# Attention and two MoE layers in one program: second copies of q and k made by transfers, and four more weights converted in the third token block

## The chip, the cores and the metric

One Trainium2 chip, one core. The metric is the device time of one execution of the program in microseconds (us). TensorE (PE) multiplies; VectorE (DVE), ScalarE (ACT) and GpSimd (POOL) do elementwise work; SyncE (SP) issues every transfer of this kernel, in the order in which they stand on its queue.

## The reference

```python
def _attn_ref(q, k, v, f):                      # 4 batches, 8 heads, 576 tokens, 64 wide
    scores = scale * np.matmul(q, k.transpose(0, 1, 3, 2))
    cum = np.cumsum(np.log(np.clip(f, 0.0001, 1.0)), axis=-1)
    scores = np.where(causal, -1e9, scores + cum[..., :, None] - cum[..., None, :])
    ...
    return np.matmul(attn, v)
def _moe_ref(x, w_in, w_out):                   # 2304 tokens, 512 -> 2048 -> 512
    h = x @ w_in
    return (h * np.clip(h + 3.0, 0.0, 6.0) / 6.0) @ w_out
def _moe2_ref(x, w_in, w_out):
    h = x @ w_in
    g = np.maximum(h, 0.0) + np.log1p(np.exp(-np.abs(h)))
    return g @ w_out
```

The output is the second MoE of the first MoE of the attention. The weights of both MoEs arrive as 64-bit floats, so each 128x512 piece of them is loaded as two 32-bit words an element (512 KB) and converted on the chip to float32.

## The kernel before

**Precision.** Most products run in the faster rounded format (fp32r): an operand is split into a rounded part and a rest, and three products (rounded x rounded, rounded x rest, rest x rounded) are summed. For the scores of attention the split is laid out along the partitions: tile QA holds 64 rows of rounded q and 64 rows of its rest; KA holds rounded k twice; KB holds the rest of k, and QB once more the rounded q, each with rows for the decay. One score product is KA x QA plus KB x QB. So the rounded q must stand in QA and in QB, and the rounded k must stand twice in KA: these are the second copies.

**Attention.** Heads go in 16 pairs, two heads (0 and 1) to a pair. The first four pairs use plain float32 (`whole`); from the fifth on `qk_job` (L588) makes the split for a pair: VectorE transposes the raw tile (L599), ScalarE rounds each head (`hi`, L629), VectorE makes the rest (`lo`, L632), and `dup` (L638 to L645) makes the second copy: by a transfer (L641), on ScalarE (L643) or on VectorE (L645). The tiles of the seventh to the sixteenth pair are one set (`z` is 0), so a pair's head is rounded only when the same head of the pair before has had its scores. Then `s_job` multiplies (L685), VectorE finds the row minimum (L701), ScalarE takes exponentials (L710), TensorE transposes them (L776), and `pv_job` multiplies by v (L846).

**First MoE.** Tokens go in blocks of 512 (the fifth has 256); each block runs through 16 slices `ft` of the hidden width, with `moe1_g1` (L1296), the activation (ScalarE L1336, VectorE L1338, the split of its result L1316 or L1317 and L1319) and `moe1_g2` (L1359). Blocks one to three run on TensorE between the pieces of attention; blocks four and five run together after attention has ended.

**Second MoE.** It works with sums of quarter matrices (seven products in place of eight): `step_a` (L1412) and `step_b` (L1513). Its weights have to be converted from 64 bits (ScalarE L1017, VectorE L1019 and L1020), summed (L1104), and split (ScalarE L1133, GpSimd or VectorE L1136) before. Some of them are converted early, in blocks two and three of the first MoE, by `early2`, and stored to `wf_dram` (L1070); the table `early` (L1563) says which goes with which slice. In blocks four and five `weights2` loads these as float32 (L1088, 256 KB); those not in the table are loaded raw (L1002, 512 KB) and converted there.

**What sets the order.** Each operation is an `Op` with one or more ways (an engine and a cost), a due time `at`, and what it depends on. `Work.order` (L148) takes them one by one: on each engine the one that can start first, and of ways the one that would end first. It writes the order of all queues, so a change of one operation's ways moves others. Every engine then works through its queue in order. For `dup` the three ways carry a surcharge: 2800 ns for the transfer, 469.53 ns on ScalarE, none on VectorE.

Of the kernel before, what the change touches and what calls it, by code (L numbers as in the profile page):

```python
# [48 lines left out]
    NZ=6,  # L49
# [56 lines left out]
class Work:  # L106
# [11 lines left out]
    def op(self, ways, fn=None, r=(), w=(), after=(), at=0.0, banks=(), hold=(), free=(), nbytes=0, name="", seq=None, from_=0.0, rows=1.0):  # L118


        o = Op()
        o.ways = [ways] if isinstance(ways, tuple) else list(ways)
        o.at, o.banks, o.hold, o.free, o.nbytes, o.name = at, list(banks), hold, free, nbytes, name
        o.deps, o.succ, o.est, o.eng = {}, [], 1000.0 * from_, None
        o.early, o.rows = self.mark, rows
        for b in o.banks:
            b.users += 1
        r, w = list(r) + o.banks, list(w)
        for t in r:
            if t in self.writer:  # L130
                o.deps[self.writer[t]] = 1
        for t in w:
            for d in [self.writer.get(t)] + self.readers.get(t, []):
                if d is not None:
                    o.deps.setdefault(d, 1)
        for t in after:
            for d in [self.writer.get(t)] + self.readers.get(t, []):
                if d is not None:
                    o.deps.setdefault(d, 0)
        if seq:  # L140
            if seq in self.writer:
                o.deps.setdefault(self.writer[seq], 0)
            self.writer[seq] = o
        for t in r:
            self.readers.setdefault(t, []).append(o)
        for t in w:
            self.writer[t] = o
            self.readers[t] = []  # L148
        self.ops.append(o)
        return o  # L150
# [123 lines left out]
def attention_two_moe_kernel(  # L274
# [19 lines left out]
    B, H, S, D = q.shape  # L294
    NT, DM = out.shape
    NC = DM // P
    NF = moe_w_out.shape[0] // P
# [32 lines left out]
    op = wk.op  # L330
# [6 lines left out]
    def act(n, psum, extra=0):  # L337
        return 0.833 * n + (50 if psum else 93) + 93 * extra

    def dve(n, fast=False, extra=0):  # L340
        return (0.52 if fast else 1.04) * n + 67 + 61 * extra
# [10 lines left out]
    def dma(fn, nbytes, n=1, **kw):  # L352
        return op(("sp", 520.0 * n, fn), nbytes=nbytes, **kw)
# [9 lines left out]
    def moe_at(t, ft):  # L363

        t = min(t, LAST_B - 1)
        return BLK[t] + (BLK[t + 1] - BLK[t]) * (ft / NF) ** (K["cA"] if t == 0 else 1.0)
# [44 lines left out]
    NE, NS, NZ = K["NE"], K["NS"], K["NZ"]  # L411
# [91 lines left out]
    def qz(n):  # L503

        return (NZ - n) % 2 if n < NZ else 0
# [83 lines left out]
    def qk_job(b, hp, nm, at):  # L589

        pn = b * HP + hp
        whole = pn < NS
        z = qz(pn)
        tz = 1 if pn < NZ and nm == "kr" else 0
        x = "Q" if nm == "qr" else "K"
        A = x + "A"
        if not whole:
            wk.mark = ("w",) if tz else ()
            op(("dve", dve(S), lambda: nc.vector.transpose(T["t"][tz], raws[nm])), r=[(nm, 0), (nm, 1), "early"], w=[("t", tz)], at=at, name="T" + x)  # L599
        wk.mark = ("s", "w") if whole else ("w",) if z or tz else ()  # L600
        new = ["early", "set1"] if z and not whole else ["early"]
        for i in range(2):
            a, c = (0, D) if i == 0 else (D, 0)
            bh = b * H + 2 * hp + i
            if whole:
                op(("dve", dve(S), lambda i=i, a=a: nc.vector.transpose(T[x][i][0:D], raws[nm][a:a + D])),
                   r=[(nm, i), "early"], w=[(x + "F", i)], at=at, name=f"T{x}{i}")

                def row(i=i):
                    o = D if nm == "qr" else D + 32  # L610
                    return T[x][i][o:o + 1]

                def cum(bh=bh):
                    return T["vr"][cz].rearrange("p j h d -> p (j h d)")[bh:bh + 1, 0:S] if bh < 2 else cum_dram[bh:bh + 1]

                if bh == 0:
                    op([("act", act(S, False), lambda: nc.scalar.activation(out=row(0), in_=cum(0), func=ACTF.Copy)),
                        ("dve", dve(S, True), lambda: nc.vector.tensor_copy(row(0), cum(0)))],
                       r=["early", ("vr", cz)], w=[(x + "Fd", i)], at=-1.5, name="dec0")
                else:  # L620
                    dma(lambda row=row, cum=cum: nc.sync.dma_start(out=row(), in_=cum()), 4 * S,
                        r=["early", ("vr", cz) if bh < 2 else "cum"], w=[(x + "Fd", i)], at=at - K["xl"], name="dec")
                continue

            def to(y, o, i=i):
                return T[x + y][z][i][o:o + D]

            def hi(a=a, to=to):
                nc.scalar.activation(out=to("A", a), in_=T["t"][tz][a:a + D], func=ACTF.Copy)  # L629

            def lo(a=a, c=c, to=to):
                nc.vector.tensor_tensor(  # L632
                    to("A", c) if nm == "qr" else to("B", 0), T["t"][tz][a:a + D], to("A", a).bitcast(F32), op=ALU.subtract)

            op(("act", act(S, False), hi), r=new + [("t", tz)], w=[(A, z, i)], at=at, name=f"{A}{i}hi")
            op(("dve", dve(S), lo), r=[("t", tz), (A, z, i)], w=[("QAl" if nm == "qr" else "KB", z, i)], at=at, name=f"{A}{i}lo")

            def dup(e, a=a, c=c, to=to):  # L638
                o, y = to("B", 0) if nm == "qr" else to("A", c), to("A", a).bitcast(F32)
                if e is nc.sync:  # L640
                    e.dma_start(out=o.bitcast(F32), in_=y)  # L641
                elif e is nc.scalar:
                    e.activation(out=o, in_=y, func=ACTF.Copy)  # L643
                else:
                    e.tensor_copy(o, y)  # L645

            def dec(i=i, bh=bh):
                o = T["QB"][z][i][D:D + 2] if nm == "qr" else T["KB"][z][i][D + 2:D + 4]
                nc.sync.dma_start(out=o.bitcast(F32), in_=dec_dram[bh])

            ways = [("sp", 520.0, lambda f=dup: f(nc.sync), 2800.0),
                    ("act", act(S, False), lambda f=dup: f(nc.scalar), K["dupa"]),
                    ("dve", dve(S, True), lambda f=dup: f(nc.vector), K["dupd"])]
            op(ways, nbytes=4 * D * S, r=[(A, z, i)], w=[("QB" if nm == "qr" else "KAl", z, i)], at=at, name=f"dup{A}{i}")
            dma(dec, 8 * S, r=["dec"] + new, w=[(x + "Bd", z, i)], at=at - K["xl"])

    def s_job(pn, i, idx, at):
# [264 lines left out]
    def attention():  # L922
# [5 lines left out]
        for nm in ("qr", "kr"):  # L928
            qk_job(*specs[0], nm, 0.0)
            load_qk(nm, *specs[1], K["lq1"])  # L930
        prev = None
        for n in range(len(specs) + 1):
            for i in range(2):
# [26 lines left out]
                if i == 1 and n + 1 < len(specs):  # L960
                    for nm in ("qr", "kr"):
                        qk_job(*specs[n + 1], nm, when(0.95))
                        if n + 2 < len(specs):
                            load_qk(nm, *specs[n + 2], when(1.0))
# [595 lines left out]
        for o in range(2):  # L1560
            weights(o, ft, moe_at(0, ft) - K["cv"] + o * 2)

    early = {(1 + n // 8, n % 8 * 2): (1, n) for n in range(NF)} | {(1 + n // 4, n % 4 * 2 + 9): (0, n) for n in range(NF // 2)} if wide else {}  # L1563
    late2 = [(o, ft) for o in range(2) for ft in range(NF) if wide and (o, ft) not in early.values()]
    units = [(t, ft) for t in range(NB - 2) for ft in range(NF)]
    units += [(t, ft) for ft in range(NF) for t in (NB - 2, NB - 1)]
    for n in range(len(units) + 1):
        if n < len(units):
            t, ft = units[n]
            if (t, ft) == (NB - 2, 0):  # L1570
# [3 lines left out]
                at = moe_at(t, 0) - K["xl"]  # L1574
# [6 lines left out]
            if ft == NF - 1 and t + 1 < NB - 1:  # L1581

                at = moe_at(t + 1, 0) - K["xl"]
# [85 lines left out]
```

## Time and profile before

| | us |
|---|---|
| runs | 1009.79, 1010.3, 1008.93; median 1009.79 |
| the profiled execution | 1006.66 |
| its span, first to last instruction | 1004.7 |
| busy in the span: TensorE | 972.6 |
| VectorE | 801.8 |
| ScalarE | 590.1 |
| GpSimd | 249.2 |

The granted clock of TensorE is 1.00 (2.4 GHz) in all stretches shown below. Where the stages lie: the first MoE's block one is written out (L1387, L1388) at 240 to 245 us, block two at 369 to 372, block three at 486 to 498, blocks four and five at 625 to 629; `step_a` (L1412) runs from 628 to 820 and `step_b` (L1513) from 812 to 999. The last pair of heads is normalized (L879) at 472. How to read a page: busy time is the time in which an engine had an instruction; idle time counts only on the engine that sets the end, here mostly TensorE; a wait row says which instruction ended an idle time. TensorE's instructions overlap, so their mean duration is longer than the step from one to the next.

### The profile page before, as it was taken

To read this page: it belongs to the slowest core of one execution; us is meant where nothing else is said; L and a number is where in the kernel's file an instruction comes from. 1 tells how busy PE (TensorE), PEld (TensorE's weight loads), DVE (VectorE), ACT (ScalarE), POOL (GpSimd) and SP (SyncE) were. 2 spreads that over 40 slices of the span, in tenths; PEclk is the share of its full clock that TensorE was granted. 3 is DMA by queue.
4 is the path that set the end of the run, shared out by engine and by line. 5 is a ranking of instruction groups with operands and counts; after the bars stand their busy time and mean duration, and the time that the engine had idled before them with its cause. 6 is when DMAs were issued, how large, how long until landed. Compare 5 with 4: busy or idle time off the path is not lost.

```text
span 1004.7 us, 17646 instructions
## 1 busy us (share of the span) xinstructions
PE 972.6 (97%) x6116; PEld 847.3 (84%) x6116; DVE 801.8 (80%) x1615; ACT 590.1 (59%) x1295; POOL 249.2 (25%) x242
## 2 busy tenths in 40 slices
PE   8998999999999999999999999999999999999997
PEld 6565777778888788888888887899999999999997
DVE  8789878898989777886685876878787768888885
ACT  6998777777676556774344545655565544343342
POOL 2222232310000100000454642210010317554442
PEclk9999999999999999999999999999999999999999
DMA  6775544554654426542664751543425994444442
GB/s 139 171 189 150 141 129 117 144 142 99 169 153 162 100 88 180 147 132 83 215 213 145 251 163 46 170 167 132 143 103 197 332 354 125 125 143 134 124 121 72
DMA packets 192065, 153.46 MB, mean 153 GB/s; under 512 B 108220, under 2 KB 163932, under 8 KB 191080
## 3 DMA queue, kind: packets, MB, share of 16 engines
q1 hardware_dynamic: 191976, 152.34, 50.7%
q8 instruction: 48, 0.79, 0.3%
q14 instruction: 41, 0.34, 0.1%
HBM read 99.68 MB, written 52.47 MB: 151 GB/s over the span
## 4 chain that ended last, share of the span: by engine, by line
PE 69%; DVE 16%; issue 4%; DMA 4%; ACT 2%; POOL 2%; SPq 1%; DVEq 0%; POOLq 0%; ACTq 0%
PE bank L1513 16%; PE bank L1296 14%; PE bank L1412 14%; PE bank L1359 13%; PE bank L685 5%; PE bank L846 4%; PE bank L776 4%; DVE MX L1319 2%; DVE GT L1338 1%; DMA st<-in_moe_w_in_dram 1%; DVE p L701 1%; DVE st L1020 1%; SPq L535 1%; DMA st<-in_moe_w_out_dram 1%; DVE KB L632 1%
## 5 line engine op out<-in xcount | busy, mean ns | idle before, releaser
L1296 PE MATMUL bank<-MX,W 128*128 128x512 f32 x768 | 224.2, 402 | 9.1 <-DVE GT L1338 6.0
L1359 PE MATMUL bank<-MX,W 128*128 128x512 f32 (+1 forms) x688 | 186.3, 380 | 0.0
L1296 PEld LDWEIGHTS bank<-MX,W 128*128 128x128 f32 x768 | 132.1, 189 | 31.0 <-DVE GT L1338 7.7
L1359 PEld LDWEIGHTS bank<-MX,W 128*128 128x128 f32 x688 | 121.5, 188 | 22.1 <-DVE MX L1319 0.3
L1513 PE MATMUL bank<-rW,rW 128*128 128x256 f32 x1134 | 138.7, 283 | 1.4 <-POOL rW L1136 0.8
L1513 PEld LDWEIGHTS bank<-rW,rW 128*128 128x128 f32 x1134 | 136.8, 191 | 2.2 <-POOL rW L1136 1.0
L1412 PE MATMUL bank<-XO,rW 128*128 128x288 f32 x672 | 92.8, 298 | 3.0 <-DVE HY L1430 1.2
L1412 PEld LDWEIGHTS bank<-XO,rW 128*128 128x128 f32 x672 | 90.3, 188 | 4.9 <-DVE rBW L1430 1.8
L710 ACT ACTIVATE p<-p,stats 64x64 f32<-64x64 f32 (+4 forms) x130 | 72.0, 555 | 31.5 <-DVE stats L701 30.7
L1492 ACT ACTIVATE rW<-st 128x512 fp32r<-128x512 f32 (+1 forms) x72 | 36.9, 518 | 77.3 <-PE bank L1513 50.9
L1336 ACT ACTIVATE GT<-bank,three 128x512 f32<-128x512 f32 x80 | 51.4, 643 | 37.0 <-DVE MX L1319 16.2
L1412 PE MATMUL bank<-MX,rW 128*128 128x288 f32 x480 | 70.2, 297 | 1.3 <-DVE HY L1430 1.0
L1412 PEld LDWEIGHTS bank<-MX,rW 128*128 128x128 f32 x480 | 65.8, 188 | 2.1 <-DVE HY L1430 1.2
L1033 POOL TENSOR_TENSOR W<-st,W 128x512 fp32r<-128x512 f32 x24 | 33.2, 1387 | 135.3 <-ACT W L1032 118.8
L581 POOL TENSOR_TENSOR V<-vr,V 128x640 fp32r<-128x640 f32 x10 | 16.3, 1629 | 195.9 <-ACT V L577 168.5
L1319 DVE TENSOR_TENSOR MX<-GT,MX 128x512 fp32r<-128x512 f32 (+1 forms) x69 | 53.7, 784 | 11.5 <-ACT MX L1316 10.8
L1496 POOL TENSOR_TENSOR rW<-st,rW 128x256 fp32r<-128x256 f32 (+1 forms) x35 | 42.1, 1206 | 79.7 <-ACT rW L1492 61.7
L1338 DVE SCALAR_TENSOR_TENSOR GT<-GT,bank 128x512 f32<-128x512 f32 x80 | 49.9, 629 | 14.3 <-ACT GT L1336 13.3
L701 DVE CUSTOM_DVE_ANT_0 p<-bank,bar 64x64 f32<-64x64 f32 (+4 forms) x130 | 51.6, 421 | 11.4 <-PE bank L685 10.1
L776 PEld LDWEIGHTS bank<-ident,p 128*128 128x128 f32 x390 | 46.6, 140 | 14.7 <-DVE ptl L816 1.6
L811 ACT ACTIVATE pth<-bank 128x320 fp32r<-128x320 f32 (+2 forms) x100 | 42.3, 432 | 27.5 <-PE bank L776 21.4
L776 PE MATMUL bank<-ident,p 128*128 128x128 f32 x390 | 57.7, 274 | 0.6 <-ACT p L730 0.2
(215 smaller groups left out, 2042.4 us busy)
## 6 DMA issues: line engine op xcount, KB each, us to landing
st<-g_dram SPq DMA_DIRECT2D x36, 512.0 KB
st<-in_moe_w_out_dram SPq DMA_DIRECT2D x32, 512.0 KB
st<-in_moe_w_in_dram SPq DMA_DIRECT2D x30, 512.0 KB
wo_dram<-XO SPq DMA_DIRECT2D x49, 256.0 KB
g_dram<-HY SPq DMA_DIRECT2D x16, 576.0 KB
g_dram<-rBW SPq DMA_DIRECT2D x16, 576.0 KB
rW<-wo_dram SPq DMA_DIRECT2D x5, 1792.0 KB
wf_dram<-st SPq DMA_DIRECT2D x24, 256.0 KB
```

Source lines behind the costliest of these rows:

```text
L685: nc.tensor.matmul(acc[:r, o:o + c - a], qs[:, q0:q0 + r], ks[:, a:c], start=(n == 0 and ti == todo[-1][0]), stop=(n == len(ops) - 1), ski ...
L701: nc.vector.tensor_tensor_reduce(out=T["P"][par][ti][:r, a:c], in0=bank[bk.i][:r, o:o + c - a], in1=bar[:r, b0:b0 + c - a], op0=ALU.add, o ...
L710: nc.scalar.activation(out=pt, in_=pt, func=ACTF.Exp, scale=-1.0, bias=sv[:r, 0, ti:ti + 1], accum_out=sv[:r, 1, ti:ti + 1],)
L776: nc.tensor.transpose(acc[:, p0:p0 + P], T["P"][par][ti][:, k0:k0 + P], ident)
L811: nc.scalar.activation(out=place("PTH", j, ks, a, c), in_=src(), func=ACTF.Copy)
L1296: nc.tensor.matmul(bank[bk.i][:, 0:n], w[:, c], x[:, c, 0:n], start=(c == 0 and p == 0), stop=(c == NC - 1 and p == 2))
L1319: op(("dve", dve(n), lambda: nc.vector.tensor_tensor(t(glt), g, t(ght).bitcast(F32), op=ALU.subtract)), r=[("g", i), ("gh", i3)], w=[("gl" ...
L1336: op(("act", act(n, True, 1), lambda: nc.scalar.activation(out=g, in_=bank[bk.i][:, 0:n], func=ACTF.Relu, bias=three)), r=["three"], banks ...
L1338: op(("dve", dve(n), lambda: nc.vector.scalar_tensor_tensor(out=g, in0=g, scalar=6.0, in1=bank[bk.i][:, 0:n], op0=ALU.min, op1=ALU.mult)), ...
L1359: nc.tensor.matmul(bank[b][:, o:o + n], w[:, c * P:(c + 1) * P], x, start=(ft == 0 and p == 0 and o == 0), stop=(ft == NF - 1 and p == 2), ...
L1412: nc.tensor.matmul(bank[bks[b].i][:, 0:HA], wa[u][:, c], xa[v][:, c], start=(nm in ("P1", "P2", "P5") and c == 0 and y == 0), stop=(c == 1 ...
L1513: nc.tensor.matmul(bank[bks[b].i][:, o * 256:(o + 1) * 256], ga[u], wa[v], start=(p == 0 and o == 0 and y == 0), stop=(p == NPR - 1 and y ...
```

## The change

```diff
@@ qk_job, ways of dup @@
             ways = [("sp", 520.0, lambda f=dup: f(nc.sync), 2800.0),
                     ("act", act(S, False), lambda f=dup: f(nc.scalar), K["dupa"]),
                     ("dve", dve(S, True), lambda f=dup: f(nc.vector), K["dupd"])]
-            op(ways, nbytes=4 * D * S, ...)
+            op(ways if pn < NZ else ways[:1], nbytes=4 * D * S, ...)
@@ table of early conversions @@
-    early = {(1 + n // 8, n % 8 * 2): (1, n) for n in range(NF)} | {(1 + n // 4, n % 4 * 2 + 9): (0, n) for n in range(NF // 2)} if wide else {}
+    early = {(1 + n // 8, n % 8 * 2): (1, n) for n in range(NF)} | {(1 + (n + 4) // 8, (n + 4) % 8 * 2 + 1): (0, n) for n in range(3 * NF // 4)} if wide else {}
```

`NZ` is 6, so from the seventh pair of heads on the second copies have the transfer as their only way. The built program has 40 of these transfers in place of one; the copies on VectorE fall from 39 to 8 (those of pairs five and six), those on ScalarE from 8 to none. The table now has twelve first weights in place of eight: numbers 8 to 11 are new, and 4 to 7 stay in block three. Block three then has 16 conversions in place of 12, one with each slice, and blocks four and five have four in place of eight.

Other work moves along with this. In the first block four activation splits go from ScalarE (L1316) to VectorE (L1317), and in blocks four and five seven weight rests go from GpSimd to VectorE (L1136), while two weight sums (L1104) go the other way.

VectorE's queue at the ninth pair, before (QB_164 and KA_165 are the second copies of q, head 1, and k, head 0; GT is the first MoE's activation):

```order
L632 TENSOR_TENSOR QA_162<-qkt_169,QA_162 64x576
L645 CAST QB_164<-QA_162 64x576
L599 STREAM_TRANSPOSE qkt_169<-kr 128x576
L861 TENSOR_TENSOR xs<-bank_76,xs 64x256
L1338 SCALAR_TENSOR_TENSOR GT<-GT,bank_71 128x512
L632 TENSOR_TENSOR KB_167<-qkt_169,KA_165 64x576
L645 CAST KA_165<-KA_165 64x576
L632 TENSOR_TENSOR KB_168<-qkt_169,KA_166 64x576
```

The same place now:

```order
L632 TENSOR_TENSOR QA_162<-qkt_169,QA_162 64x576
L861 TENSOR_TENSOR xs<-bank_76,xs 64x256
L599 STREAM_TRANSPOSE qkt_169<-kr 128x576
L861 TENSOR_TENSOR xs<-bank_75,xs 64x320
L725 TENSOR_SCALAR stats_149<-stats_149 128x10
L726 RECIPROCAL stats_149<-stats_149 128x10
L632 TENSOR_TENSOR KB_167<-qkt_169,KA_165 64x576
L1019 TENSOR_SCALAR st_170<-st_170 128x512
L632 TENSOR_TENSOR KB_168<-qkt_169,KA_166 64x576
L1020 SCALAR_TENSOR_TENSOR st_170<-st_170 128x512
L1338 SCALAR_TENSOR_TENSOR GT<-GT,bank_71 128x512
```

Both copies are gone, and the activation L1338 of that slice stands behind the rests of k and a weight conversion.

SyncE's queue at the eighth pair now, a piece of the difference (L649 loads decay rows, L1002 loads raw weights, L733 stores the row sums, L535 loads the next pair's k; the rows marked + stood elsewhere or are new):

```order
+L649 DMA QB_164<-dec_dram 2x576
+L649 DMA KB_168<-dec_dram 2x576
+L641 DMA QB_164<-QA_162 64x576
+L1002 DMA st_170<-in_moe_w_in_dram 128x4x256
 L733 DMA inv_dram_93<-p_152 10x128
+L535 DMA kr<-in_k_dram 32x18x32 x4
+L1002 DMA st_171<-in_moe_w_out_dram 128x1024
+L641 DMA KA_165<-KA_165 64x576
+L641 DMA KA_166<-KA_166 64x576
 L745 DMA ivb<-inv_dram_93 64x64
```

The copies of k stand behind the loads of the next k and behind a weight load that waits for its staging buffer.

VectorE's queue in blocks four and five, a piece of the difference (st_170 is a staging buffer of a weight that was converted here before):

```order
 L1136 TENSOR_TENSOR XO<-XT,XO 128x256
-L1019 TENSOR_SCALAR st_170<-st_170 128x512
-L1020 SCALAR_TENSOR_TENSOR st_170<-st_170 128x512
 L1338 SCALAR_TENSOR_TENSOR GT<-GT,bank_71 128x256
 L1104 TENSOR_TENSOR XT<-XO 128x256
 L1319 TENSOR_TENSOR SB<-GT,SB 128x512
```

The two instructions of a conversion that stood between a weight rest and the activation are gone.

## Rows read from the trace of the kernel before

**Rows 1.** Stretches: us; busy us (instructions) PE, PEld, DVE, ACT, POOL; clock; DMA share; GB/s
```profile
105.00:245.00 140.00, 134.73 (x703) 105.51 (x702) 117.41 (x265) 103.93 (x234) 32.98 (x23) 1.00 0.48 129
245.00:480.00 235.00, 232.92 (x1273) 194.24 (x1272) 192.95 (x467) 150.46 (x347) 12.79 (x8) 1.00 0.49 138
480.00:628.00 148.00, 142.15 (x789) 120.77 (x788) 108.86 (x163) 66.64 (x146) 66.85 (x74) 1.00 0.53 170
```

**Rows 2.** TensorE's waits, 105 to 245 us: total us, times, longest us
```profile
PE bank L1296 <- DVE GT L1338: 3.3, 2, 2.0
```

**Rows 3.** TensorE's waits, 480 to 628 us
```profile
PE bank L1296 <- DVE GT L1338: 4.7, 7, 1.8
```

**Rows 4.** Second copies, groups by line, 105 to 440 us: xcount | busy us, mean ns
```profile
L645 DVE CAST QB<-QA 64x576 fp32r<-64x576 f32 x16 | 8.3, 521 | 0.2
L645 DVE CAST KA<-KA 64x576 fp32r<-64x576 f32 x15 | 6.8, 454 | 0.3
```

**Rows 5.** VectorE in order of time at the ninth pair: start, us, instruction
```profile
197.24 1.56 DVE L645 CAST QB<-QA 64x576 fp32r<-64x576 f32 x1
...
200.09 0.69 DVE L1338 SCALAR_TENSOR_TENSOR GT<-GT,bank 128x512 f32<-128x512 f32 x1
```

**Rows 6.** TensorE in order of time there: in brackets, idle before and what ended it
```profile
200.84 0.96 PE L1296 MATMUL bank<-MX,W 128*128 128x512 f32 x3 [1.35 <-DVE GT L1338]
```

**Rows 7.** GpSimd in order of time there
```profile
197.17 1.32 POOL L1033 TENSOR_TENSOR W<-st,W 128x512 fp32r<-128x512 f32 x1 [0.46 <-ACT W L1032]
```

**Rows 8.** VectorE in order of time at the eighth pair
```profile
163.24 0.45 DVE L645 CAST KA<-KA 64x576 fp32r<-64x576 f32 x1
...
165.50 0.69 DVE L1338 SCALAR_TENSOR_TENSOR GT<-GT,bank 128x512 f32<-128x512 f32 x1
```

**Rows 9.** VectorE in order of time, blocks four and five
```profile
558.40 1.03 DVE L1020 SCALAR_TENSOR_TENSOR st<-st 128x512 uint32<-128x512 uint32 x1
559.36 0.41 DVE L1338 SCALAR_TENSOR_TENSOR GT<-GT,bank 128x256 f32<-128x256 f32 x1
```

**Rows 10.** TensorE in order of time, blocks four and five
```profile
559.82 0.62 PE L1296 MATMUL bank<-SB,W 128*128 128x256 f32 x3 [0.86 <-DVE GT L1338]
...
582.38 0.96 PE L1296 MATMUL bank<-MX,W 128*128 128x512 f32 x3 [0.70 <-DVE GT L1338]
```

**Rows 11.** Weight conversions, groups by line, 320 to 480 us
```profile
L1020 DVE SCALAR_TENSOR_TENSOR st<-st 128x512 uint32<-128x512 uint32 x14 | 9.6, 683 | 0.4
L1019 DVE TENSOR_SCALAR st<-st 128x512 uint32<-128x512 uint32 x14 | 5.9, 419 | 0.1
```

**Rows 12.** Weight rests on VectorE, group by line, whole span
```profile
L1136 DVE TENSOR_TENSOR XO<-XT,XO 128x256 fp32r<-128x256 f32 x13 | 9.7, 752 | 0.0
```

**Rows 13.** ScalarE, then SyncE, in order of time at the one copy by transfer
```profile
344.54 0.69 ACT L629 ACTIVATE QA<-qkt 64x576 fp32r<-64x576 f32 x1 [3.09 <-PE bank L685]
...
345.32 0.51 SPq L641 DMA_DIRECT2D QB<-QA  x1
```

**Rows 14.** Transfers, 345.3 to 347.9 us, busy tenths in 40 slices of 0.065 us
```profile
DMA  0002000000000000009699689896410000000000
```

**Rows 15.** ScalarE rounding k, twelfth and sixteenth pair (two heads a row)
```profile
295.63 1.37 ACT L629 ACTIVATE KA<-qkt 64x576 fp32r<-64x576 f32 x2
...
434.61 1.39 ACT L629 ACTIVATE KA<-qkt 64x576 fp32r<-64x576 f32 x2 [0.16 <-DVE qkt L599]
```

**Rows 16.** TensorE, first scores of head 0 of these two pairs
```profile
299.14 0.39 PE L685 MATMUL bank<-KA,QA 128*128 128x192 f32 x2
...
441.19 0.37 PE L685 MATMUL bank<-KA,QA 128*128 128x192 f32 x2
```

**Rows 17.** The chain of waits, 150 to 215 us: raw weight loads, from issue to landing
```profile
154.00 4.33 DMA st<-in_moe_w_out_dram
...
162.35 3.86 DMA st<-in_moe_w_in_dram
```

**Rows 18.** SyncE's waits, whole span
```profile
SPq L1002 <- POOL W L1033: 21.0, 13, 5.2
```

More of the change, by code (lines that the diff above doesn't have):

```diff
@@ L653, in qk_job @@
                     ("dve", dve(S, True), lambda f=dup: f(nc.vector), K["dupd"])]
-            op(ways, nbytes=4 * D * S, r=[(A, z, i)], w=[("QB" if nm == "qr" else "KAl", z, i)], at=at, name=f"dup{A}{i}")
+            op(ways if pn < NZ else ways[:1], nbytes=4 * D * S, r=[(A, z, i)], w=[("QB" if nm == "qr" else "KAl", z, i)], at=at, name=f"dup{A}{i}")
             dma(dec, 8 * S, r=["dec"] + new, w=[(x + "Bd", z, i)], at=at - K["xl"])
```

## The prediction

> **What bounds the kernel now.** I read the stretches first. From 105 us on the change acts; the reader is to see that TensorE is busy nearly all of each stretch, so only its idle time can be won: 140.00 - 134.73 = 5.3 us from 105 to 245, 235.00 - 232.92 = 2.1 us from 245 to 480, 148.00 - 142.15 = 5.9 us from 480 to 628 [rows 1]. VectorE is busy 117.41 of the first 140 us: it is the next engine there. Then I read who ends TensorE's idle time. In the first stretch 3.3 us are two waits for the activation L1338 on VectorE [rows 2], in the last 4.7 us are seven such waits [rows 3]. So the first-MoE activation, late on VectorE, is what TensorE waits for where it waits at all; in the middle stretch, where attention's later half runs, there is almost nothing to wait for. Last I looked for what stands ahead of L1338 in VectorE's order of time.
>
> **The change, part by part.** The sum is made against the profiled execution, 1006.66 us; the median of the runs, 1009.79, stands 3.1 us above it, and I add that at the end.
>
> *Copies that leave VectorE.* From 105 us on VectorE makes 16 + 15 = 31 second copies, 8.3 + 6.8 = 15.1 us [rows 4]; all go. (ScalarE's eight go too; no wait of TensorE named in rows 2 or 3 ends on ScalarE, so I price them at nothing.) What counts is a copy ahead of a late L1338. There are two. At the ninth pair a copy of 1.56 us stands two short instructions ahead of L1338 [rows 5], and L1338 ended 1.35 us of idle time [rows 6]: without the copy the whole wait can go. At the eighth pair a copy of 0.45 us stands one instruction ahead of L1338 [rows 8], which ended the longest wait, 2.0 us [rows 2]: 0.45 can go. I take 1.35 + 0.45 = 1.8 us. The ends are 0, since the planner fills the room (four activation splits of the first block move onto VectorE, about 4 x 0.45 = 1.8 us by the nearest row, a cast [rows 4], and in the new order other work stands ahead of L1338), and 5.3, all the idle time of the stretch.
>
> *The middle stretch.* VectorE loses copies and gains four conversions of 0.683 + 0.419 = 1.10 us [rows 11], 4.4 us, beside as many on ScalarE. All of it lies beside TensorE, which is idle 2.1 us here; I take a gain of 0.3, with ends 0 and 2.1. What hides the conversions is that VectorE is busy 192.95 of 235 us [rows 1]; with that cover gone each would cost its 1.10. The four transfers in and four out lie on queues whose DMA share is 0.49 [rows 1]; nobody waits for them until block four.
>
> *Four conversions that leave blocks four and five.* Two of their instructions stand just ahead of an L1338: 1.03 us before the L1338 of 559.36 [rows 9], which ended 0.86 us of idle time, and another ahead of the wait of 0.70 [rows 10]. That is 1.56 us of waits that lose their cause. But seven weight rests come onto VectorE in the same blocks, 7 x 0.752 = 5.3 us by the nearest row [rows 12], and the conversions that leave are worth 4 x 1.10 = 4.4 at their usual price [rows 11]; VectorE's sum does not fall. I take half, 0.8 us. Ends: a loss of 5.3 - 4.4 = 0.9, and 4.7, all waits for L1338 [rows 3]. Loads of 256 KB in place of 512 KB are worth nothing more, since no wait in rows 3 ends on a transfer.
>
> *What the copies cost as transfers.* The trace has one. Its source was rounded by 344.54 + 0.69 = 345.23; SyncE issued it at 345.32 and spent 0.51 us [rows 13]; its packets ended in the 30th slice of 0.065 us, at 347.25 [rows 14]: 2.0 us after the rounding, with the queues idle otherwise. Is that in time? The tightest is the first k copy, head 0: at the twelfth pair it is rounded at 295.63 + 1.37/2 = 296.3 [rows 15] and its scores start at 299.14 [rows 16], 2.8 us later; at the sixteenth pair 435.3 and 441.19 leave 5.9. Ten copies are of this kind; the other thirty are made a pair's head earlier than they are read. So an undisturbed copy costs TensorE nothing. Behind a raw weight load it does: such a load takes 4.33 or 3.86 us from issue to landing [rows 17], and the copy's own packets 12 slices, 0.8 us [rows 14], so up to 5.1 us, 2.3 too late at the twelfth pair and in time at the sixteenth. I take 0.5 us for all ten, with ends 0 and 2.3. SyncE's 39 x 0.51 = 20 us of issuing lie beside its waits; loads stand queued well ahead of their use, and if that cover goes it is the third rival below.
>
> *Sum.* 1.8 + 0.3 + 0.8 - 0.5 = 2.4 us less: 1004.3 against the profiled execution, and 1007.4 as a median of runs.
>
> **A rule against the first term.** The copy at 197.24 took 1.56 us, while the copies of k take 0.454 on average [rows 4], and GpSimd worked on a weight rest from 197.17 for 1.32 us [rows 7]. The Trainium skill (GPSIMD Engine Reference, section 1, Specifications) says that GpSimd shares its SBUF interface with VectorE and contends with VectorE instructions that run in a two-port mode or have two SBUF inputs. The row agrees: the lengthening came while GpSimd worked. That makes a rival, the second below, since 1.1 of the 1.56 us would not leave with the copy but pass to the next VectorE instruction.
>
> **The rivals.**
> First, *the idle time only moves*. The planner rewrites all queues: of the waits that I remove, some other instruction is late next (a weight conversion or the rests of k, which now stand ahead of L1338). For it: VectorE is 84% busy from 105 to 245 [rows 1], and TensorE's order moves too. Against: 15.1 us less on VectorE. Time: no change, 1009.8.
> Second, *the lengthening passes on*: the ninth pair's wait shrinks by the copy's usual 0.45 in place of 1.35 [rows 4, 6], the first term is 0.9, the sum 1.5 us: 1008.3.
> Third, and slower: *the k copies come late by SyncE's queue*. In the new order a raw weight load stands directly ahead of the first k copy at four of the ten pairs (the eighth, twelfth, thirteenth and sixteenth), and such a load waits for GpSimd to give its staging buffer back: 21.0 us in 13 waits, 1.6 each, at most 5.2 [rows 18]. The copy would then land 1.6 + 4.33 + 0.8 = 6.7 us after the rounding: 3.9 too late at the twelfth pair and 0.8 at the others if they have the sixteenth's room, 3.9 + 3 x 0.8 = 6.3 us of TensorE's time. Against the gains of 2.9 that is 3.4 us slower: 1013.2. It decides once the copies are late by 2.9 + 2.0 = 4.9 us together. For it: TensorE works in order, and the middle stretch has no other idle time to hide this in. Against: the new TensorE order puts the scores later at such pairs, and buffers are often free.
> That the change does not do what it says is no rival: the new queues show 40 transfers, and four raw loads fewer in blocks four and five.
>
> **How the numbers follow.** A measurement of this kernel can tell about 0.2%, 2.0 us, from no change, so faster is below 1007.8 and slower above 1011.8. Forecast 0.46, taken as faster, its own range 1004 to 1007.8; idle time moves 0.22 and lengthening passes on 0.10, both within 0.2%; late copies 0.22. The range reaches down to 1002.0, where the first and third terms come out at three times the size taken (2.6 x 3 = 7.8 us less), and up to 1013.2, the price of the late copies, rounded to 1013.0.
>
> **What would show it.** Right: L645 has 8 instructions left; from 105 to 245 TensorE's waits for L1338 fall from 3.3 us to below 2, from 480 to 628 from 4.7 to about 4; the copies land about 2 to 3 us after the rounding; TensorE's waits at L685 stay below 1 us from 245 to 480. Wrong: waits of TensorE at L685 for a transfer of several us (third rival); waits for L1338 of the old size at other places (first); long L632 beside GpSimd at the ninth pair (second).

## The result, and the profile after

| us | before | changed |
|---|---|---|
| median of runs (6 each, taken together) | 1010.04 | 1001.05 |
| ratio, 95% interval | | 0.991 [0.989, 0.9931] |
| the profiled execution | 1006.66 | 1000.53 |
| its span | 1004.7 | 998.7 |

Faster by 9.0 us in the medians, where 2.4 were forecast: the direction was right, and the time lies just below the range's lower end of 1002.0. The two profiled executions differ by 6.1 us. The stretches of the changed kernel, columns as in [rows 1]:

```profile
105.00:245.00 140.00, 138.31 (x730) 109.46 (x729) 115.55 (x263) 103.46 (x235) 33.94 (x24) 1.00 0.60 155
245.00:480.00 235.00, 233.55 (x1264) 193.38 (x1262) 188.45 (x453) 147.44 (x340) 12.31 (x8) 1.00 0.59 165
480.00:628.00 148.00, 143.34 (x816) 123.72 (x816) 102.75 (x163) 67.74 (x146) 65.68 (x70) 1.00 0.52 168
```

TensorE's idle time in the first stretch falls from 5.3 to 140.00 - 138.31 = 1.7 us. The waits of TensorE in that stretch, all that the view lists (total us, times, longest):

```profile
PE bank L776 <- DVE ptl L816: 1.3, 2, 0.9
PE bank L776 <- ACT p L730: 0.3, 1, 0.3
```

The two waits for the activation L1338 [rows 2] are gone; what is left are short waits in attention, at L776. The same view from 480 to 628 us:

```profile
PE bank L1296 <- DVE GT L1338: 4.3, 4, 1.8
PE bank L1359 <- DVE SB L1319: 0.2, 1, 0.2
```

Against [rows 3] this looks like 0.4 us, but the window has moved: everything behind the first block comes about 4 us earlier, so that other work falls into it. To compare like with like I count TensorE's matmuls in their order, each at the median step that its kind takes in the kernel before, and ask when the same sum is reached. Changed minus before, in us, at five points of the time of before (the last column is 9 us before the end):

| run | 113 | 278 | 555 | 705 | 991 |
|---|---|---|---|---|---|
| changed kernel | +0.9 | -3.8 | -2.5 | -5.5 | -6.1 |
| changed kernel, second profile | +1.0 | -3.7 | -0.5 | -3.2 | -4.0 |
| before, second profile | +0.2 | +0.2 | +0.4 | +0.8 | +1.8 |

The first block gives 0.9 + 3.8 = 4.7 us, the middle takes back 1.3, and blocks four and five give 3.0 (all of it before 600 us). The +0.9 arises before 24 us, where nothing was changed; the section on the hardware tells of it.

### The profile page after: what moved, and what is told of

Same layout as the page of the kernel before. It is cut to its first block, busy times and chain, and to the rows that moved or that the text cites. A ratio compares the mean times of both kernels' runs of the same rounds, so it can differ in the third digit from the quotient of the medians.

```text
span 998.7 us, 17738 instructions
## 1 busy us (share of the span) xinstructions
PE 972.6 (97%) x6116; PEld 847.8 (85%) x6116; DVE 785.1 (79%) x1593; ACT 583.1 (58%) x1281; POOL 248.1 (25%) x239
## 4 chain that ended last, share of the span: by engine, by line
PE 80%; DVE 11%; issue 3%; DMA 2%; ACT 2%; POOL 1%; SPq 0%; DVEq 0%; ACTq 0%; POOLq 0%
PE bank L1359 18%; PE bank L1296 17%; PE bank L1513 16%; PE bank L1412 14%; PE bank L685 6%; PE bank L846 5%; PE bank L776 4%; DMA st<-in_moe_w_out_dram 1%; DVE st L1020 1%; DVE GT L1338 1%; DVE rBW L1458 1%; DMA st<-in_moe_w_in_dram 1%; DVE HY L1430 1%; DVE MX L1319 0%; DMA st<-g_dram 0%
## 5 line engine op out<-in xcount | busy, mean ns | idle before, releaser
L1338 DVE SCALAR_TENSOR_TENSOR GT<-GT,bank 128x512 f32<-128x512 f32 x80 | 50.1, 630 | 15.9 <-ACT GT L1336 15.3
L1319 DVE TENSOR_TENSOR MX<-GT,MX 128x512 fp32r<-128x512 f32 (+1 forms) x69 | 50.5, 735 | 15.0 <-ACT MX L1316 14.2
L776 PEld LDWEIGHTS bank<-ident,p 128*128 128x128 f32 x390 | 46.4, 141 | 16.3 <-DVE ptl L816 3.0
L776 PE MATMUL bank<-ident,p 128*128 128x128 f32 x390 | 58.0, 276 | 1.5 <-DVE ptl L816 1.3
```

Of the source, the lines that this page charges most:

```text
L776: nc.tensor.transpose(acc[:, p0:p0 + P], T["P"][par][ti][:, k0:k0 + P], ident)
L1319: op(("dve", dve(n), lambda: nc.vector.tensor_tensor(t(glt), g, t(ght).bitcast(F32), op=ALU.subtract)), r=[("g", i), ("gh", i3)], w=[("gl" ...
L1338: op(("dve", dve(n), lambda: nc.vector.scalar_tensor_tensor(out=g, in0=g, scalar=6.0, in1=bank[bk.i][:, 0:n], op0=ALU.min, op1=ALU.mult)), ...
```

## The experiments

"Theory A" below is that the gain is the sum of two separate effects: copies that leave VectorE win TensorE's idle time in the first block, and conversions that leave blocks four and five win it there. The table at the end of this section has all profiles by the measure above; "block one" is the difference of the columns 278 and 113, "four and five" that of 705 and 555.

### Each part alone

copies_only has the first edit of the change alone, early_only the second alone.

> Part one alone: the second copies from the seventh pair on go by transfers, the table of early conversions is that of before. Theory A (two separate gains: the copies leave VectorE in the first block, about -6 of the -9 us; the four conversions leave blocks four and five, about -3): 1003 to 1005 us, TensorE's waits for L1338 from 105 to 245 us gone, those of 490 to 620 as before (about 4.7 us). Theory B (a new order of the queues, which only both parts together give): within 1 us of before, 1009 to 1011. Theory C (all of it is the copies): 1000 to 1002.

> Part two alone: four more conversions in the third block, the copies with their three ways as before. Theory A: 1006 to 1008 us, the first stretch (105 to 245 us) as before with about 5 us of idle time of TensorE, the gain of 2 to 3 us between 490 and 620. Theory B: within 1 us of before. Theory C: within 1 us of before. If the conversions are all of it: 1000 to 1002.

Measured: copies_only 1006.01 us median, ratio 0.9947 [0.9928, 0.9966]; early_only 1008.27, 0.9958 [0.9939, 0.9977]. TensorE's waits in copies_only, from 105 to 245 us and then from 480 to 628:

```profile
PE bank L776 <- DVE ptl L816: 1.3, 2, 0.9
PE bank L729 <- DVE stats L726: 0.4, 1, 0.4
```
```profile
PE bank L1296 <- DVE GT L1338: 5.2, 7, 1.8
```

And in early_only, in the same two stretches:

```profile
PE bank L1296 <- DVE GT L1338: 3.3, 2, 2.0
```
```profile
PE bank L1296 <- DVE GT L1338: 4.1, 3, 1.8
```

Each part does its own work and nothing of the other's. In block one copies_only gains 4.3 us and early_only nothing; in blocks four and five it is 0.1 and 4.0. The ratios' savings of 0.0053 and 0.0042 add up to 0.0095, beside 0.009 for both together (each is known to about 0.002). Theory A stands; that only both parts together make an order that gains is out.

### The two kernels once more

> The kernel before, unchanged, for a second profiled execution. The first one was 3.4 us below the median of the runs. If the usual runs of before lose their further 3 us at the same waits for L1338, this profile shows about 8 in place of 5 us of idle time of TensorE from 105 to 245, or about 8 in place of 6 from 480 to 628. If the 3 us come from the granted clock of TensorE in the first 60 us or from loading, the idle time is as it was and the difference lies before 105 us.

> The changed kernel, unchanged, for a second profiled execution. Expected near 1001 us, with under 2.5 us of idle time of TensorE from 105 to 245 and about 5 from 480 to 628; a difference of more than 1 us to its first profile would show which stretch varies from run to run.

Single runs, 1008.34 and 1002.8 us. Neither guess on before was right in full: its waits are the same to 0.1 us from 105 to 245 and 5.2 in place of 4.7 from 480 on, with the clock at 1.00 to 60 us. The profiles of before are among its quickest executions. A straight line through the 150 executions of this study that have a clock on record, with one slope for all kernels, gives 0.8 us for each 0.001 of mean granted clock, and at a clock of 1.000 it puts before at 1007.3 and the changed kernel at 1000.0. So 7.3 of the 9.0 us are there at an equal clock, and the rest goes with the mean clock of the runs (median 0.995 of before and 0.997 of the changed kernel's); whether the change has a part in that clock stays open.

### Where the copies count, and where they may go

copies_block1 and copies_late have transfers for the pairs seven to ten or eleven to sixteen alone; copies_on_act has ScalarE as the only way; copies_twice has the transfers and, beside them, a cast of the same size on VectorE into a dead tile (40 casts, nine more than the copies that VectorE made before). All four keep the table of before.

```diff
-ways if pn < NZ else ways[:1]
+ways[:1] if NZ <= pn < 10 else ways            # copies_block1
+ways[:1] if pn >= 10 else ways                 # copies_late
+ways if pn < NZ else ways[1:2]                 # copies_on_act
```

> Only the copies of the seventh to the tenth pair go by transfers (those beside the first block), the later pairs keep three ways, the table of early conversions is that of before. Theory A (the gain of the copies is idle time of TensorE in the first block, 4.2 us with all pairs): the gain from 105 to 260 us is there as with all pairs, 4 to 5 us, and the time is that of the copies alone, near 1006 us. Theory B (any new order gives a gain somewhere): the stretch from 105 to 260 gives 0 to 2 us. Theory C (the relief of the middle stretch counts): 0 to 1 us there and 1009 to 1011 in all.

> Only the copies of the eleventh to the sixteenth pair go by transfers, the table is that of before. Theory A: no gain, 1009 to 1012 us, TensorE's idle time from 105 to 245 stays near 5 us. Theory C: 1005 to 1007 us. If late transfers cost anything, it shows here without a gain beside it: waits of TensorE at L685 for a transfer, up to 2 us.

> The copies from the seventh pair on have ScalarE as their only way in place of the transfer, the table is that of before. Theory A (what counts is that VectorE is relieved, wherever the copies go): the gain from 105 to 260 us is 3 to 5 us as with transfers, less what ScalarE, 74 per cent busy there, makes late; in all 1005 to 1008 us. Rival (the order of SyncE's queue, which the transfers change, gives the gain): no gain, 1009 to 1012.

> The copies go by transfers as in the run with the copies alone, and besides VectorE casts each rounded tile once more into the raw transposed tile, which is dead by then: SyncE has the transfers, VectorE has the load of before and a little more (40 casts in place of 31). If the load of VectorE is what the copies took away: the gain from 105 to 260 us (4.2 us) shrinks to 0 to 2, 1008 to 1012 us in all. Rival (the transfers' order on SyncE and the new order of TensorE give the gain): 4 us stay, 1005 to 1007 us.

Measured: 1005.84 us, 0.9958 [0.9935, 0.9982]; 1012.08, 0.9999 [0.9978, 1.0019]; 1010.97, 0.999 [0.997, 1.001]; 1012.19, 1.0017 [0.9995, 1.0039]. The copies of four pairs give all of the copies' gain (block one: 5.0 us); the later transfers alone give nothing that can be told. On ScalarE the copies win nothing at all. ScalarE's groups of copies from 105 to 245 us there (xcount | busy us, mean ns), and TensorE's waits from 155 to 205:

```profile
L643 ACT ACTIVATE KA<-KA 64x576 fp32r<-64x576 f32 x8 | 5.5, 685 | 0.2
L643 ACT ACTIVATE QB<-QA 64x576 fp32r<-64x576 f32 x8 | 5.5, 684 | 0.2
```
```profile
PE bank L685 <- DVE xs L861: 1.1, 1, 1.1
PE bank L776 <- DVE xs L861: 0.9, 1, 0.9
```

The waits for L1338 are gone here as well, but others stand in their place, and block one loses 0.3 us. With the transfers and VectorE's load put back and a little more (copies_twice) it loses 2.3; the longest wait there, and the stretch of TensorE right behind it (columns as in [rows 1], the other engines left out), are

```profile
PE bank L685 <- ACT W L1032: 1.5, 1, 1.5
```
```profile
175.00:180.00 5.00, 4.80 (x18) 0.66 0.78 231
```

At a clock of 0.66 these 5 us hold 5 x 0.34 = 1.7 us less work, so by this estimate the order itself loses about 0.6.

So transfers in SyncE's queue and a new order win nothing by themselves: the copies have to leave VectorE, and may not come onto ScalarE.

In the profile of copies_late the first block gains 1.5 us, though it changes no copy there. This is no new order: the instructions of TensorE, VectorE, ScalarE, GpSimd and SyncE stand in before's order up to 244 us. All of the gain is at the longest wait, which is 0.4 us here in place of 2.0. VectorE, GpSimd and TensorE there:

```profile
160.12 0.65 DVE L1020 SCALAR_TENSOR_TENSOR st<-st 128x512 uint32<-128x512 uint32 x1
...
161.25 1.31 DVE L632 TENSOR_TENSOR KB<-qkt,KA 64x576 fp32r<-64x576 f32 x1
...
163.06 0.75 DVE L632 TENSOR_TENSOR KB<-qkt,KA 64x576 fp32r<-64x576 f32 x1
```
```profile
160.07 1.86 POOL L1033 TENSOR_TENSOR W<-st,W 128x512 fp32r<-128x512 f32 x1 [6.17 <-ACT W L1032]
163.23 1.74 POOL L1033 TENSOR_TENSOR BW<-st,W 128x512 fp32r<-128x512 f32 x1 [1.29 <-ACT W L1032]
```
```profile
PE bank L1296 <- DVE GT L1338: 0.4, 1, 0.4
```

In before the instructions at 160.20 and 163.73 took 1.80 and 1.74 us; here GpSimd's two rests are the longer ones. So the same order can gain or lose 1.6 us at this place from one execution to the next: the other profiles with this order and full rests (before, its second one, early_only, convs_cut_before) have the 2.0 us, and copies_cut_before has 1.6.

### What a wait for L1338 was made of

Three kernels keep the order of before, row for row on every engine, and make some instructions nearly free. rests_cut_before (and rests_cut_after, the same in the changed kernel) cuts GpSimd's weight rests of slices 5 to 11:

```diff
-nc.gpsimd.tensor_tensor(WT[o, ft][1], w, WT[o, ft][0].bitcast(F32), op=ALU.subtract)
+the same on [:, 0:32] if 5 <= ft < FW; the rest of those tiles set to 0 by nc.gpsimd.memset while ft is 1 to 4
```

> The kernel before in its own order on every engine, with GpSimd's weight rests of slices 5 to 11 of the first MoE cut to 32 of 512 columns (the other columns are zero, so the rests of these weights are left out of the products). VectorE's instructions that were lengthened beside such a rest (1.1 us each at 160.20, 163.73, 195.56 and 197.24) should take their usual time. If these lengthenings, standing in an unbroken row of VectorE's work, made the waits for L1338: from 105 to 245 TensorE's idle time falls from 5.3 to 2.5 us or less, the waits for L1338 from 3.3 to under 1. If the number of copies alone made them: 4.5 to 5.3 us stay.

> The same cut in the changed kernel. By either theory little is left to win there: TensorE's idle time from 105 to 245 goes from 1.7 to 1 to 1.7 us. A larger gain would mean that the lengthenings cost TensorE time without a wait that is put down to them.

First VectorE and GpSimd in the kernel before, ahead of the wait of 2.0 us at 166.2 (start, us, instruction); VectorE had worked without a break since 156.4:

```profile
160.20 1.80 DVE L1020 SCALAR_TENSOR_TENSOR st<-st 128x512 uint32<-128x512 uint32 x1
...
163.73 1.74 DVE L632 TENSOR_TENSOR KB<-qkt,KA 64x576 fp32r<-64x576 f32 x1
```
```profile
160.13 1.31 POOL L1033 TENSOR_TENSOR W<-st,W 128x512 fp32r<-128x512 f32 x1 [6.17 <-ACT W L1032]
163.28 1.56 POOL L1033 TENSOR_TENSOR BW<-st,W 128x512 fp32r<-128x512 f32 x1 [1.83 <-ACT W L1032]
```

And the same instructions of rests_cut_before, with GpSimd, and TensorE's waits from 155 to 205 us:

```profile
158.10 0.75 DVE L1020 SCALAR_TENSOR_TENSOR st<-st 128x512 uint32<-128x512 uint32 x1
...
160.09 0.45 DVE L645 CAST KA<-KA 64x576 fp32r<-64x576 f32 x1
160.58 0.75 DVE L632 TENSOR_TENSOR KB<-qkt,KA 64x576 fp32r<-64x576 f32 x1
```
```profile
158.04 0.26 POOL L1033 TENSOR_TENSOR W<-st,W 128x32 fp32r<-128x32 f32 x1 [7.36 <-ACT W L1032]
161.25 0.26 POOL L1033 TENSOR_TENSOR BW<-st,W 128x32 fp32r<-128x32 f32 x1 [2.95 <-issue]
```
```profile
PE bank L1296 <- DVE GT L1338: 1.4, 1, 1.4
```

The copy still stands ahead of L1338 and takes its 0.45 us, and the wait of 2.0 us is gone: the two lengthenings of 1.05 and 0.99 us had made it. The wait at the ninth pair stays at 1.4, since there the rests belong to later slices, which were not cut (I had expected 160.20, 163.73, 195.56 and 197.24 to shorten; only the first two did). So TensorE's idle time from 105 to 245 is 140.00 - 136.85 = 3.2 us, where 2.5 or less was expected. Block one gains 2.6 us; another 2.7 are gained before 105 us, 1.0 of them near 78 us, ahead of the first rest that is cut (93 us), which no run explains. rests_cut_after (a single run of 999.22 us) shows the waits left in the changed kernel halved: 140.00 - 139.24 = 0.8 us of idle time in place of 1.7.

copies_cut_before cuts the copies themselves, from the eighth pair on:

```diff
-o, y = to("B", 0) if nm == "qr" else to("A", c), to("A", a).bitcast(F32)
+o, y = the same, on [:, 0:32] if pn > NZ and e is not nc.sync
```

> The kernel before in its own order on every engine, with the second copies of the eighth to the sixteenth pair cut to 32 of 576 columns where VectorE or ScalarE makes them (the other columns keep what the seventh pair left, so the scores are not those of the reference). By the prediction's step (only the copies directly ahead of a late L1338 count) TensorE gains 1.8 us from 105 to 245. If the lengthening beside GpSimd passes on to VectorE's next instruction: about 0.9 us. If the shorter queue alone gives what the change gave: 3.5 to 4.7 us, with no transfer and no new order.

A single run, 1010.02 us, of which 4.1 arose before 24 us. TensorE's waits from 155 to 205 us, and VectorE and GpSimd at the ninth pair:

```profile
PE bank L1296 <- DVE GT L1338: 2.7, 2, 1.6
```
```profile
199.28 1.76 DVE L632 TENSOR_TENSOR QA<-qkt,QA 64x576 fp32r<-64x576 f32 x1
200.96 1.29 DVE L645 CAST QB<-QA 64x32 fp32r<-64x32 f32 x1
...
204.90 0.18 DVE L645 CAST KA<-KA 64x32 fp32r<-64x32 f32 x1
```
```profile
200.88 1.33 POOL L1033 TENSOR_TENSOR W<-st,W 128x512 fp32r<-128x512 f32 x1 [0.46 <-ACT W L1032]
```

A copy of 32 columns takes 0.18 us alone and 1.29 beside GpSimd, 0.27 less than the whole one [rows 5]. So a copy that leaves takes its own 0.45 or less with it and not the 1.56 that its row shows. In the old order the copies' own time is worth 1.0 us to 245 us (progress +4.1 to +3.1) and 1.8 to 278, not 4.7.

convs_cut_before does this with the second conversion instruction of first weights 8 to 11 in blocks four and five:

```diff
-out=words(i)[:, 0].bitcast(U32) if dense else low(), in0=up(), scalar=3, in1=low(),
+the same on [0:32] of 512 if m == 1 and o == 0 and 8 <= ft < 12
```

> The kernel before in its own order on every engine, with VectorE's second conversion instruction (L1020, 0.69 us) of first weights 8 to 11, those that the change moves to block three, cut to 32 of 512 columns (these weights are then not the reference's). If VectorE's time in these conversions made the waits between 555 and 600 us: 2 to 3 of the 3.3 us are gained there. If it is their loads (512 in place of 256 KB) or the new order: under 1 us.

A single run, 1010.33 us, of which 4.2 arose before 24 us. Blocks four and five gain 2.2 us, in the old order and with the loads as they were; TensorE's waits from 480 to 628 us:

```profile
PE bank L1296 <- DVE GT L1338: 3.3, 5, 1.8
```

The four cut instructions take 0.54, 0.18, 0.76 and 0.18 us in place of 1.03, 0.68, 1.25 and 0.68, so 2.0 us of VectorE's time are gone and TensorE gains about as much. So VectorE's own time gives at least 2.2 of the 3.0 to 4.0 us that the conversions gave when they left (changed kernel and early_only); smaller loads or a new order are not needed for that part, and whether they have a share in the rest is not shown.

### Further along both edits

all_early converts all sixteen first weights early; all_early_copies_all adds transfers for the fifth and sixth pair, all_early_block1 has them for pairs seven to ten alone.

```diff
-| {(1 + (n + 4) // 8, (n + 4) % 8 * 2 + 1): (0, n) for n in range(3 * NF // 4)}
+| {(1 + n // 8, n % 8 * 2 + 1): (0, n) for n in range(NF)}
```

> The changed kernel with all sixteen first weights converted early, eight with each of blocks two and three: no conversion of a first weight is left for blocks four and five, four more in the second block. If conversions leaving blocks four and five go on to pay at the rate of the four before (about 3 us for four): 997 to 999 us. If the waits that are left there (4.3 us for L1338) are not behind conversions: 1000 to 1002 us, the same as the changed kernel. If block two has no room for four more: over 1003 us.

> All sixteen first weights early, and the copies of the fifth and sixth pair go by transfers too (eight more). If the copies pay where VectorE is busiest, some 0.5 to 2 us more than all sixteen early alone, 994 to 996 us; if these two pairs come before their loads can (from 60 to 105 us TensorE is idle 3.5 us), 996 to 1000.

> All sixteen first weights early, and transfers only for the copies of the seventh to the tenth pair; the later pairs have three ways again. If the late transfers cost 0.5 us here too and nothing else: 995 to 997 us, the same as with all transfers within what can be told. If the early conversions, which crowd VectorE in blocks two and three, need the room that the late transfers make: 998 to 1001 us.

Measured: all_early 996.32 us (994.45 to 998.07, 4 runs), ratio 0.9842 [0.981, 0.9874], below the changed kernel's interval: the best version found. all_early_copies_all 1002.15, 0.9917 [0.9894, 0.994]; all_early_block1 1000.07, 0.99 [0.9875, 0.9924]. In all_early blocks four and five give 8.2 us; from 480 to 628 us TensorE waits no more than

```profile
PE bank L1296 <- DVE GT L1338: 2.0, 2, 1.8
```

Transfers for the fifth and sixth pair win 3.1 us where these pairs run, between 24 and 105 us (+1.0 to -2.1 against before), but spoil block one, which loses 1.7 us in place of gaining 4.2: TensorE's waits from 105 to 155 us in all_early_copies_all are

```profile
PE bank L846 <- DVE stats L701: 1.5, 2, 0.9
PE bank L776 <- DVE ptl L816: 1.5, 1, 1.5
PE bank L685 <- ACT pt L802: 0.7, 2, 0.5
```

None of them names a transfer; why the planner's order is worse there was not tried further. Without the late transfers all_early_block1 is the slower one (1000.07, upper end of what I had expected): the middle loses 2.0 us there, and about nothing in all_early once its fall of the clock behind 526 us is taken off (last section). That VectorE has both the early conversions and the late copies in blocks two and three is the likely reason; no run separates it.

| run | 113 | 278 | 555 | 705 | 991 | block one | four and five |
|---|---|---|---|---|---|---|---|
| copies_only | +2.6 | -1.7 | +1.0 | +0.9 | +2.2 | -4.3 | -0.1 |
| early_only | +4.2 | +4.2 | +4.9 | +0.9 | +1.7 | 0.0 | -4.0 |
| copies_block1 | +1.0 | -4.0 | -2.9 | -2.7 | -3.4 | -5.0 | +0.2 |
| copies_late | -0.1 | -1.6 | +0.6 | +1.4 | +1.5 | -1.5 | +0.8 |
| copies_on_act | +1.0 | +1.3 | +2.4 | +2.3 | +2.9 | +0.3 | -0.1 |
| copies_twice | +1.8 | +4.1 | +6.8 | +7.7 | +7.0 | +2.3 | +0.9 |
| rests_cut_before | -1.6 | -4.2 | -3.9 | -3.6 | -2.3 | -2.6 | +0.3 |
| rests_cut_after | +1.5 | -4.3 | -4.1 | -7.1 | -7.3 | -5.8 | -3.0 |
| copies_cut_before | +4.1 | +2.3 | +1.6 | +1.8 | +3.5 | -1.8 | +0.2 |
| convs_cut_before | +4.2 | +4.5 | +4.6 | +2.4 | +3.7 | +0.3 | -2.2 |
| all_early | +2.6 | -1.6 | +0.1 | -8.1 | -8.8 | -4.2 | -8.2 |
| all_early_copies_all | -0.9 | +0.8 | +3.0 | -4.7 | -4.3 | +1.7 | -7.7 |
| all_early_block1 | +0.5 | -4.1 | -2.1 | -10.0 | -9.3 | -4.6 | -7.9 |

## Why the prediction was right in sign and wrong in size

*Copies that leave VectorE: 1.8 taken, 4.3 to 4.7 came.* The step that failed is "what counts is a copy ahead of a late L1338. There are two". It took 0.45 us for the longest wait and 1.35 for the other, and both were wrongly put down to copies. The wait of 2.0 us came from two lengthenings of 1.05 and 0.99 us in one unbroken row of VectorE's work, which I read no further back than the copy: with the rests cut it is gone, and with GpSimd held in place of VectorE (copies_late) it is 0.4, the copy standing where it stood both times. At the ninth pair the second rival had the mechanism right: the 1.1 us beside GpSimd do not leave with the copy, and in the old order the copies' own time gives 1.0 us by 245. It was wrong that the lengthening then lands on TensorE. The changed kernel has nearly as many lengthened instructions as before from 105 to 245 (11 that take over 0.3 us more than the median of their kind, 9.1 us too much together; before 12 and 9.8), but VectorE's next idle time ends within 4.5 us behind ten of the eleven, where in before it ended only 9.4 and 19.3 us behind the first one ahead of either wait, and no wait for L1338 is left. About 1 to 1.8 us of the gain are thus the copies' time, and the other some 3 us came only together with the new order that the planner made with the room. So the term lay near its upper end, 5.3. That the order alone would give the 3 us is not shown: with the room taken again on ScalarE or VectorE there was no gain.

*The middle stretch: 0.3 taken, a loss of 1.3 came.* copies_block1, which has no late transfers, loses 1.1 there too, and the views name no wait for a transfer; so it is more likely the order than the copies, which no run separates further.

*Four conversions that leave blocks four and five: 0.8 taken, about 3 came.* The step "VectorE's sum does not fall. I take half" failed. VectorE's conversions from 480 to 628 us, before and then after:

```profile
L1019 DVE TENSOR_SCALAR st<-st 128x512 uint32<-128x512 uint32 x5 | 3.2, 638 | 2.7 <-DMA st<-in_moe_w_in_dram 2.7
L1020 DVE SCALAR_TENSOR_TENSOR st<-st 128x512 uint32<-128x512 uint32 x4 | 3.1, 772 | 0.4 <-ACT st L1017 0.3
L1020 DVE SCALAR_TENSOR_TENSOR HY<-HY 128x512 uint32<-128x512 uint32 x2 | 1.9, 966 | 0.0
L1019 DVE TENSOR_SCALAR HY<-HY 128x512 uint32<-128x512 uint32 x2 | 1.4, 696 | 1.8 <-DMA HY<-in_moe_w_in_dram 1.8
```
```profile
L1020 DVE SCALAR_TENSOR_TENSOR st<-st 128x512 uint32<-128x512 uint32 x4 | 2.8, 692 | 0.5 <-ACT st L1017 0.3
L1019 DVE TENSOR_SCALAR st<-st 128x512 uint32<-128x512 uint32 x4 | 1.7, 424 | 2.5 <-DMA st<-in_moe_w_in_dram 2.5
```

They fall by 9.6 - 4.5 = 5.1 us in this window, and by more in truth, since three instructions of before lie behind 628 us. The eight that left stood between 557 and 582 us and took 7.0 us, not the 4.4 of [rows 11], because five of them were lengthened:

```profile
557.34 0.96 DVE L1019 TENSOR_SCALAR st<-st 128x512 uint32<-128x512 uint32 x1
...
562.75 0.96 DVE L1019 TENSOR_SCALAR st<-st 128x512 uint32<-128x512 uint32 x1
...
576.97 1.25 DVE L1020 SCALAR_TENSOR_TENSOR HY<-HY 128x512 uint32<-128x512 uint32 x1
...
579.28 0.96 DVE L1019 TENSOR_SCALAR HY<-HY 128x512 uint32<-128x512 uint32 x1
```

The fifth is the 1.03 us of [rows 9]. And the seven rests that came did not stand ahead of a late L1338: all four waits between 555 and 600 went, two of which [rows 10] I had named and halved. Those four are 2.0 us in the view of waits, while the progress gains 3.3 us there: a recorded wait understates what TensorE loses.

*What the copies cost as transfers: 0.5 taken, nothing came that the views show.* From 245 to 480 us TensorE waits 0.3 us at L685 for L1338, 0.2 for L816, and for no transfer, as "what would show it" had it (below 1 us). When the copies landed behind their rounding is not read here. The third rival, copies late behind raw weight loads, did not occur: SyncE's transfers keep their order, but no k copy was late enough to be waited for.

*The median against the profiled execution.* I added 3.1 us to both kernels alike. By the line through all executions, 1.7 us of the 9.0 go with the runs' granted clock, a term that the sum against one profile didn't have. At an equal clock the gain of 7.3 us would have ended at 1002.5 from the median of 1009.79, just inside the range; the terms above were mis-sized all the same.

## What to carry to other kernels

When TensorE waits for an engine, go back along that engine's row to its last idle time and ask of every instruction whether it took its usual time; price an instruction at its usual time, and a lengthening as something that stays when the instruction leaves. Here, with VectorE busy 84% of the stretch and a planner that can reorder, the freed time was worth nearly all of the idle time that VectorE caused, and only where it was freed without loading ScalarE, the next busiest engine. Profiles of one order can differ by a lengthening that falls on the one engine or the other, so a gain of 1.5 us in one profile needs its rows read before it is believed. Work that can be done in a stretch where the critical engine has no use for the room (conversions in blocks two and three) is worth moving completely: four gave 3 us, four more another 5.

## What the runs showed of the hardware

*GpSimd and VectorE.* VectorE's L1020 of 160.20 ended at 162.00, 0.56 us after GpSimd's rest had ended (160.13 + 1.31 = 161.44), and the copy of 32 columns above took 1.29 us beside GpSimd and 0.18 alone: the instruction stands nearly still until GpSimd is done. The Trainium skill (SBUF — State Buffer, section "SBUF: two separate sides") says this of VectorE and GpSimd: the port pair that they share is an exclusive lock, and the other "fully blocks". These rows agree, for a cast with one input as well as for instructions with two; I had used only the weaker wording of another page, which speaks of contention. In copies_late it is GpSimd that is held: its two rests took 1.86 and 1.74 us while VectorE's L1020 and second L632, at 0.65 and 0.75 us, were not lengthened.

*TensorE's granted clock.* The executions differ in their first 24 us, where early_only is not changed at all. The clock (the column after PE's busy time) is 1.00 there in the profile of before; in early_only, in two stretches of 4 us,

```profile
12.00:16.00 4.00, 4.00 (x12) 0.50 0.84 129
16.00:20.00 4.00, 4.00 (x8) 0.50 1.03 310
```

that is the lower of its two levels, 1.2 GHz in place of 2.4, though TensorE is busy throughout; from 8 to 12 us it had been busy 2.58 of 4 us in this run and 2.57 in before. It cost 4.2 us against before. The profiles of this study show a loss of 0, 1.0, 2.6 or 4.2 us in these 24 us. The clock can fall behind a long wait too. In all_early, where TensorE stood idle 1.79 us for an L1338 up to 526.0:

```profile
525.00:528.00 3.00, 1.97 (x7) 0.83 0.49 164
528.00:531.00 3.00, 3.00 (x11) 0.60 0.00 1
```

It lost 1.6 us there, and five more of the 17 profiles lost 1.5 or 1.6 at this wait (copies_only, copies_late, copies_twice, all_early_copies_all and the second one of the changed kernel); before, with the same wait of 1.78 us, kept 1.00 in both its profiles. So a wait that goes takes the chance of such a fall with it. Whether falls behind the waits at 166 and 200 us are part of why the usual runs of before have the lower mean clock is open: none of its two profiles shows one.
